# Four first loads moved to GpSimd's queue, the first batch's order list rearranged, two pieces of work moved to GpSimd

## The chip, the cores and the metric

The kernel runs on one core of a Trainium2 chip. The metric is device time in microseconds of one execution; medians of several executions are quoted, and comparisons use runs of the same rounds on the same chip. A profile is one execution under the hardware profiler; its "span" is some 1.8 us shorter than the time measured for the same execution. Names of engines: PE is TensorE, PEld its weight loads, DVE is VectorE, ACT is ScalarE, POOL is GpSimd, SP is SyncE; a name with q added (SPq) is that engine's queue of issues.

## The reference, cut to what matters

Eight batches of attention with RMS-normalised queries and keys (12 heads, 448 positions, 64 dimensions), then a layer norm and a two-layer MLP with a residual.

```python
batch, n_heads, seq, head_dim = (8, 12, 448, 64)
def rmsnorm(x, g):
    return x / np.sqrt(np.mean(x * x, axis=-1, keepdims=True) + 1e-06) * g
q_n, k_n = (rmsnorm(q, g_q), rmsnorm(k, g_k))
scores = (1.0 / np.sqrt(head_dim)) * np.matmul(q_n, k_n.transpose(0, 1, 3, 2))
attn = softmax(scores)                       # written out in the original
x = np.matmul(attn, v)                       # heads joined: (8, 448, 768)
xn = (x - mean(x)) / np.sqrt(var(x) + 1e-06) * g_ln
out = x + np.maximum(xn @ w_ch1, 0.0) @ w_ch2     # w_ch1 768x3072, w_ch2 3072x768
```

## The kernel before

Heads are worked on in pairs, and pairs are prepared in "units" (pair 0, pair 1, pairs 2 and 3, pairs 4 and 5 of batch 0, then two pairs each). To prepare a unit, its keys and queries are squared (`a`, `c`, ScalarE), summed (`d`, `e`, VectorE), put through an inverse square root (`g`, ScalarE), the keys are weighted with g_q·g_k (`i`) and split into an fp16 high part (`j`) and low part (`k`), the queries are scaled and duplicated (`l`, `m`), the values cast to fp16 (`z`, GpSimd). Then `K` and `Q` are the PE transposes of a pair's keys and queries, `S` a tile of scores with its exponential, `V` a tile of values, `N`, `X` and `R` the layer norm of batch 0 and its transposes, `U` the first MLP products. The other letters (`b`, `G`, `L`, `T`, `W`, `A`, `M`) stand for setting up a unit, later loads and small steps that the argument doesn't need. For batch 0 an explicit list gives the order in which all of this is issued to the in-order engines:

```python
DVE_KG, POOL_HI, POOL_DUP, ACT_Q = (0, 1, 2), (1, 2, 3, 4), (1, 2, 4), (0, 1)
ORDER = """
b0 a0 c0 G L4 L5 i0 j0 e0 k0 gq0 l0 b1 m0 a1 c1 K0 Q0 d0 gk0 S0.0 S0.1 i1 e1 d1 g1 z0 j1 l1 m1
k1 b2 a2 S0.2 c2 S0.3 d2 K1 e2 S0.4 V0.0 i2 S0.5 Q1 g2 j2 l2 V0.1 S0.6 S1.0 S1.1 S1.2 m2 b3
...   # cut
S6.6 X0 X1 U0 V6.5 c5 N2 X2 d5 U1 U2 R e5 V6.6 g5 j5 k5 l5 m5 z5 L7 M
""".split()
...
        def kg():                            # "i", line 229
            if u == 0:
                nc.vector.tensor_tensor(out=sh.gprod, in0=sh.gg[:, 0], in1=sh.gg[:, 1],
                                        op=ALU.mult)          # line 227
            (nc.vector if u in DVE_KG else nc.gpsimd).tensor_tensor(
                out=c["t"][1], in0=c["t"][1],
                in1=sh.gprod.unsqueeze(1).broadcast_to([128, g, D]), op=ALU.mult)

        def khi():                           # "j", line 235 or 237
            if u in POOL_HI:
                nc.gpsimd.tensor_copy(out=c["khl"][:, :, 0], in_=c["t"][1])
            else:
                nc.scalar.activation(c["khl"][:, :, 0], c["t"][1], AFT.Identity)
```

The first loads. `main` loads a pair's first 384 rows, `left` the last 64, in two halves:

```python
        for n, eng in ((0, nc.sync), (1, nc.scalar)):      # queries, keys
            main(eng, n, 0)
            left(eng, n, 0, 1)
        left(nc.scalar, 1, 1, NPAIR - 1)
        for n in range(2):
            nc.sync.dma_start(self.sh.gg[:, n], self.gs[n].unsqueeze(0).broadcast_to([128, D]))
        main(nc.sync, 1, 1)
        ...                                                # cut: SyncE's further loads
```

## Time and profile before

| what | before |
|---|---|
| time, median of 3 runs | 616.35 us (615.82 to 616.48) |
| span of the profile | 613.9 us |
| PE busy | 581.3 us, 95% |
| ScalarE busy | 362.0 us, 59% |
| VectorE busy | 289.8 us, 47% |
| GpSimd busy | 185.7 us, 30% |

Read such a table with care: PE is busy 95% over the whole run, but two thirds of its 33 us of idle time lie in the first 60 us, where the other engines are the limit, and the change concerns only that stretch. The prediction below therefore starts from the table by stretches and from what PE waited for.

### The profile page before, as it was taken

The numbers are of one execution on the slowest core, as the hardware profiler recorded it, in microseconds if no ns is written. First come the engines' busy times: TensorE is split into PE (matmuls) and PEld (weight loads), VectorE is DVE, ScalarE is ACT, GpSimd is POOL, SyncE is SP. The second block draws the span as 40 slices with busy tenths as digits, with TensorE's granted clock in tenths as the row PEclk, the third lists the DMA queues.
The fourth block names the chain that finished last, engine by engine and source line by source line (L and its number), as shares of the span: only waits on it lengthen the run. The fifth ranks groups of instructions, "written<-read, shape, count | busy, mean of one in ns | idle before, by whom it ended". The sixth has DMA issues, their size and how long they took to land.

```text
span 613.9 us, 11521 instructions
## 1 busy us (share of the span) xinstructions
PE 581.3 (95%) x4500; PEld 346.2 (56%) x4500; DVE 289.8 (47%) x615; ACT 362.0 (59%) x697; POOL 185.7 (30%) x239
## 2 busy tenths in 40 slices
PE   2777999999999999999999999999999999999995
PEld 1545566655566666655566666655566666654564
DVE  4798766733356355643356355642355422440011
ACT  4897886438754498538755398537765377114200
POOL 0646432224452155514453145605322000000000
PEclk9999999999999999999999999999999999999998
DMA  7999799655536467847659495836524330030011
GB/s 185 289 177 230 151 222 224 135 157 123 121 102 132 98 142 152 179 108 144 111 102 141 105 137 151 176 105 150 117 61 87 91 61 2 27 104 0 1 52 56
DMA packets 131661, 75.29 MB, mean 123 GB/s; under 512 B 97552, under 2 KB 121904, under 8 KB 131600
## 3 DMA queue, kind: packets, MB, share of 16 engines
q1 hardware_dynamic: 114336, 45.18, 35.2%
q0 software_dynamic: 15920, 28.71, 21.2%
q8 instruction: 37, 0.61, 0.4%
q10 hardware_dynamic: 1344, 0.59, 0.4%
q14 instruction: 24, 0.20, 0.1%
HBM read 52.36 MB, written 11.01 MB: 103 GB/s over the span
## 4 chain that ended last, share of the span: by engine, by line
PE 87%; DVE 4%; ACT 4%; issue 1%; ACTq 0%; DVEq 0%
PE psC L627 35%; PE psH L611 34%; PE psS L352 8%; PE oA L381 5%; PE oB L383 2%; ACT E L358 1%; PE psS L355 1%; PE psS L356 1%; DVE ssq L218 1%; DVE x L398 1%; ACT qn L215 1%; PE tr L316 1%; DVE khl L240 1%; DVE qU L335 0%; DVE xn L560 0%
## 5 line engine op out<-in xcount | busy, mean ns | idle before, releaser
L611 PE MATMUL psH<-xnT,w 128*128 128x512 f16 (+1 forms) x1134 | 242.1, 353 | 0.4 <-issue 0.4
L358 ACT ACTIVATE E<-psS,rr_all 128x448 f16<-128x448 f32 x336 | 207.2, 635 | 50.0 <-PE psS L352 44.1
L627 PE MATMUL psC<-w,hT 128*128 128x384 f16 (+1 forms) x1368 | 234.7, 323 | 0.0
L613 ACT ACTIVATE hT<-psH 128x512 f16<-128x512 f32 (+1 forms) x189 | 104.0, 551 | 126.2 <-PE psH L611 123.3
L627 PEld LDWEIGHTS <-hT 128*128 128x128 f16 x1368 | 127.7, 98 | 74.2
L611 PEld LDWEIGHTS <-w 128*128 128x128 f16 x1134 | 102.5, 98 | 81.4 <-issue 1.5
L352 PE MATMUL psS<-qU,kU 128*128 128x448 f16 x288 | 101.7, 360 | 8.0 <-ACT E L358 6.0
L381 PEld LDWEIGHTS <-E 128*128 128x128 f16 x1008 | 71.1, 99 | 50.3 <-issue 4.4
L229 POOL TENSOR_TENSOR qkv<-qkv,gprod 128x896 f32<-128x896 f32 x21 | 43.7, 2079 | 99.2 <-ACT khl L215 51.6
L381 PE MATMUL oA<-v,E 128*128 128x65 f16 x864 | 67.2, 194 | 0.9 <-DVE x L398 0.8
L631 DVE SCALAR_TENSOR_TENSOR x<-psC,rs_all,x 128x384 f32<-128x384 f32 x48 | 29.0, 616 | 70.8 <-PE psC L627 70.3
L396 DVE RECIPROCAL rec_all<-oA 128x6 f32<-128x6 f32 x48 | 9.3, 194 | 98.1 <-PE oA L381 98.0
L383 PE MATMUL oB<-v,E 128*128 128x65 f16 x288 | 52.1, 195 | 0.1
L127 POOL DMA_DIRECT2D qkv<-in_k_dram x14 | 11.2, 800 | 131.2 <-ACT E L358 68.6
L218 DVE TENSOR_REDUCE ssq<-khl 128x14 f32<-128x896 f32 (+1 forms) x24 | 25.5, 1064 | 43.9 <-ACT khl L215 43.8
L352 PEld LDWEIGHTS <-kU 128*128 128x128 f16 x288 | 28.2, 99 | 25.6 <-issue 7.2
L218 DVE TENSOR_REDUCE ssq<-qn 128x14 f32<-128x896 f32 (+1 forms) x25 | 26.2, 1047 | 22.9 <-ACT qn L215 22.8
L67 DVE SCALAR_TENSOR_TENSOR qn<-qkv,rq 128x256 f16<-128x256 f32 (+1 forms) x72 | 26.9, 430 | 18.7 <-ACT rq L223 18.5
L383 PEld LDWEIGHTS <-E 128*128 128x128 f16 x336 | 32.7, 97 | 0.5 <-DVE xl L403 0.2
L398 DVE TENSOR_TENSOR x<-oA,rec_all 128x384 f32<-128x384 f32 x48 | 26.8, 558 | 1.7 <-DVE rec_all L397 0.2
L240 DVE TENSOR_TENSOR khl<-qkv,khl 128x896 f16<-128x896 f32 x21 | 22.8, 1083 | 7.9 <-ACT khl L237 7.9
L540 DVE BATCH_NORM_STATS2 stat<-x 128x6 f32<-128x256 f32 x72 | 26.1, 415 | 0.7
(101 smaller groups left out, 447.9 us busy)
## 6 DMA issues: line engine op xcount, KB each, us to landing
out_dram<-x SPq DMA_DIRECT2D x20, 384.0 KB, 2.5
qkv<-in_k_dram POOLq DMA_DIRECT2D x14, 384.0 KB, 3.9
qkv<-in_q_dram POOLq DMA_DIRECT2D x14, 384.0 KB, 5.2
qkv<-in_v_dram POOLq DMA_DIRECT2D x14, 384.0 KB, 6.0
w<-in_moe_w_ch_dram POOLq DMA_DIRECT2D x3, 1536.0 KB, 12.0
w<-in_moe_w_ch_dram POOLq DMA_DIRECT2D x2, 2304.0 KB, 26.9
qkv<-in_k_dram SPq DMA_DIRECT2D x7, 384.0 KB, 5.6
qkv<-in_q_dram SPq DMA_DIRECT2D x7, 384.0 KB, 4.9
```

The lines of the kernel that those rows point to most:

```text
L218: nc.vector.tensor_reduce(out=c["ssq"][:, n], in_=c["sq", n], axis=AX.X, op=ALU.add)
L229: (nc.vector if u in DVE_KG else nc.gpsimd).tensor_tensor(out=c["t"][1], in0=c["t"][1], in1=sh.gprod.unsqueeze(1).broadcast_to([128, g, D] ...
L240: nc.vector.tensor_tensor(out=c["khl"][:, :, 1], in0=c["t"][1], in1=c["khl"][:, :, 0], op=ALU.subtract)
L352: nc.tensor.matmul(ps[:, 0:S], c["main"][:, ts(i, 128)], q[:, ts(h, S)], start=True, stop=True)
L358: nc.scalar.activation(out=c["E"][:, i], in_=ps[:, 0:S], func=AFT.Exp, scale=self.rr[:, g:g + 1], bias=EXP_BIAS)
L381: nc.tensor.matmul(oA[:, t, cs], E[:, i, ts(t, 128)], rhs, start=(i == 0 and t == 0), stop=(i == 6 and t == 2))
L383: nc.tensor.matmul(oB[:, cs], E[:, i, 320:448], rhs, start=(i == 0), stop=(i == 6))
L398: nc.vector.tensor_tensor(out=x[:, :, 128 * hp:128 * hp + 128].rearrange("p t (e d) -> p t e d", e=2), in0=oA[:, :, :, 0:D], in1=rec[:, 0: ...
L611: nc.tensor.matmul(ps[:, 0:N], sh.w1[:, dc, ts(f, 128)], xnT[:, dc, 0:N], start=(dc == 0), stop=(dc == NDC - 1))
L613: nc.scalar.activation(out=hT[:, f, 0:N], in_=ps[:, 0:N], func=AFT.Relu)
L627: nc.tensor.matmul(ps[:, 0:g[1]], hT[:, f, ts(t, 128)], sh.w2[:, f, cols], start=(f == 0), stop=(f == NFF - 1))
L631: nc.vector.scalar_tensor_tensor(out=x[:, cols], in0=ps[:, 0:g[1]], scalar=self.rs[:, b, t:t + 1], in1=x[:, cols], op0=ALU.mult, op1=ALU.add)
```

## The change

The intent is to let the first key transpose start sooner by spreading the first issues over three queues, and to feed PE better up to the first MLP by a better order of issue and by taking work from VectorE and ScalarE to GpSimd. `DVE_KG` without 2 puts the key weighting of unit 2 on GpSimd; `POOL_HI` with 5 puts the fp16 conversion of unit 5's keys there.

```diff
-DVE_KG, POOL_HI, POOL_DUP, ACT_Q = (0, 1, 2), (1, 2, 3, 4), (1, 2, 4), (0, 1)
+DVE_KG, POOL_HI, POOL_DUP, ACT_Q = (0, 1), (1, 2, 3, 4, 5), (1, 2, 4), (0, 1)
 ORDER = """
-b0 a0 c0 G L4 L5 i0 j0 e0 k0 gq0 l0 b1 m0 a1 c1 K0 Q0 d0 gk0 S0.0 S0.1 i1 e1 d1 g1 z0 j1 l1 m1
-k1 b2 a2 S0.2 c2 S0.3 d2 K1 e2 S0.4 V0.0 i2 S0.5 Q1 g2 j2 l2 V0.1 S0.6 S1.0 S1.1 S1.2 m2 b3
...  (middle cut)
-S6.6 X0 X1 U0 V6.5 c5 N2 X2 d5 U1 U2 R e5 V6.6 g5 j5 k5 l5 m5 z5 L7 M
+G b0 a0 c0 L4 L5 i0 j0 e0 k0 gq0 l0 b1 m0 a1 c1 K0 Q0 d0 gk0 S0.0 S0.1 i1 e1 d1 z0 g1 j1 l1 m1
+k1 b2 a2 S0.2 d2 c2 S0.3 S0.4 K1 V0.0 e2 i2 S0.5 Q1 g2 l2 S0.6 S1.0 j2 V0.1 S1.1 S1.2 m2 b3
...  (middle cut)
+S6.6 V6.4 X0 X1 U0 N2 d5 j5 R X2 c5 e5 g5 k5 z5 l5 L7 V6.5 U1 U2 M m5 V6.6
@@ load_first @@
-        left(nc.scalar, 1, 1, NPAIR - 1)
         for n in range(2):
-            nc.sync.dma_start(self.sh.gg[:, n], self.gs[n].unsqueeze(0).broadcast_to([128, D]))
+            nc.gpsimd.dma_start(self.sh.gg[:, n], self.gs[n].unsqueeze(0).broadcast_to([128, D]))
+        left(nc.gpsimd, 1, 1, NPAIR - 1)
```

## The prediction

> **What bounds the kernel now.** I read the busy time by stage first, because an average over the whole run hides where TensorE (PE) is idle. These are rows of the table by stretches of the kernel before (stretch, its length, busy time of PE, of PE's weight loads, of VectorE, ScalarE and GpSimd, then clock, DMA share, GB/s):
>
> ```profile
> 0.00:10.00 10.00, 0.00 (x0) 0.00 (x0) 3.56 (x14) 3.58 (x8) 0.68 (x6) 1.00 0.55 133
> 10.00:20.00 10.00, 5.46 (x32) 3.04 (x33) 7.42 (x13) 6.72 (x15) 2.80 (x5) 1.00 1.09 306
> 20.00:30.00 10.00, 9.35 (x89) 6.20 (x88) 8.02 (x11) 9.48 (x19) 6.66 (x7) 1.00 0.90 268
> 30.00:40.00 10.00, 8.58 (x115) 5.78 (x113) 9.62 (x20) 9.51 (x19) 5.43 (x7) 1.00 1.00 188
> 40.00:50.00 10.00, 7.10 (x89) 4.44 (x88) 9.59 (x21) 9.09 (x19) 5.16 (x7) 1.00 1.05 189
> 50.00:60.00 10.00, 7.36 (x108) 5.69 (x108) 8.44 (x16) 6.78 (x12) 6.33 (x5) 1.00 1.11 255
> ...
> 60.00:120.00 60.00, 56.75 (x505) 36.47 (x504) 42.04 (x84) 45.95 (x93) 19.31 (x18) 1.00 1.00 188
> 120.00:200.00 80.00, 79.44 (x567) 44.53 (x565) 36.58 (x76) 46.73 (x86) 29.77 (x39) 1.00 0.51 125
> 200.00:500.00 300.00, 300.00 (x2288) 177.81 (x2287) 138.44 (x304) 190.29 (x371) 109.58 (x147) 1.00 0.60 123
> ```
>
> From 60 us on PE is the bound: 3.3 us idle up to 120, 0.6 up to 200, none up to 500. In the first 60 us it is idle 10.0 + 4.5 + 0.7 + 1.4 + 2.9 + 2.6 = 22.1 us. PE's work is not changed, so a microsecond of PE idle saved in the first 60 us is a microsecond off the end, unless a later wait eats it. The change touches only that stage: its bound is the whole game, and 22.1 us is far more than can be had.
>
> What PE waits for there, from the table of waits (what waited, for what; us in total, times, longest):
>
> ```profile
> PE tr L313 <- DVE khl L240: 13.1, 2, 10.1
> PE psS L352 <- ACT E L358: 6.0, 18, 0.6
> ...
> DVE gprod L227 <- DMA w<-in_g_k_dram: 5.0, 1, 5.0
> ```
>
> So there are three parts: 10.1 us before the first key transpose, 3.0 us before the second (18.29), then many short waits for ScalarE's exponentials, with ScalarE 95% and VectorE 96% busy from 30 to 40. The first is a chain that I follow in the timeline (start, duration, what):
>
> ```profile
> 2.78 0.59 SPq L151 DMA_DIRECT2D w<-in_g_q_dram  x1
> 4.31 0.33 SPq L151 DMA_DIRECT2D w<-in_g_k_dram  x1
> 4.66 1.28 ACT L417 ACT_TABLE_LOAD   x1 [4.66 <-DMA hT<-in_q_dram]
> ...
> 7.84 0.23 DVE L227 TENSOR_TENSOR gprod<-w 128x64 f32<-128x64 f32 x1 [4.96 <-DMA w<-in_g_k_dram]
> ...
> 14.83 0.82 POOL L285 CAST v<-w 128x768 f16<-128x768 f32 x1 [13.52 <-DMA w<-in_v_dram]
> ...
> 17.29 0.94 DVE L240 TENSOR_TENSOR khl<-hT,khl 128x448 f16<-128x448 f32 x1 [1.16 <-POOL khl L235]
> ```
>
> The weights g_q and g_k are the fourth and fifth issues of SyncE's queue. g_k goes out at 4.31, lands 3.5 us later, the product is formed at 7.84, and key weighting (8.15), high part (8.81) and low part (9.42) follow back to back to PE's first transpose at 10.10. ScalarE meanwhile issues six key transfers until 4.63, and only then loads its table. The second wait is GpSimd's: pair 0's values land at 14.83, the conversion of unit 1's keys stands behind them (16.70), VectorE waits for that (17.29), PE for VectorE.
>
> **What the Trainium skill says.** "DMA: Bandwidth & Descriptors", section "Issuing engines are not separate DMA queues", says that spreading issues over engines saves sequencer issue time only. The trace agrees that issue time is what is scarce here: SyncE issues from 0.74 to 16.66 almost without a gap, while the DMA engines are busy only 55% in the first 10 us. Its section "Latency and other measured facts" gives a first byte at about 0.6 us on the SyncE/ScalarE path and 1 us on GpSimd's. No transfer of this size on GpSimd's queue is in the trace; the nearest, halves of left rows, take 0.60 us to issue and 3.0 us or more to land, beside 3.1 to 3.7 on SyncE's and ScalarE's. "GPSIMD Engine Reference", section "Engine selection", calls elementwise work with two inputs about twice as slow there: here the same key weighting takes 2.08 us on GpSimd and 1.08 on VectorE, so it agrees. "SBUF — State Buffer", section "Who interferes with whom", says that a VectorE instruction with two SBUF inputs contends with a GpSimd one that reads SBUF. The trace agrees: a query scaling of 1.08 us took 1.71 at 22.28 beside a GpSimd cast, and a GpSimd copy of 0.93 us took 1.66 at 24.12.
>
> **The change part by part.**
>
> *Key and query weights on GpSimd's queue.* GpSimd has finished the identity at 1.31 and has nothing until 14.83. Two issues of 0.6 to 0.9 us go out at about 1.3 and 2.1, and land 3.0 to 3.9 us later (the 3.9 is the median of whole key loads on that queue): 5.1 to 6.0, so the product is ready at about 5.4 to 6.3, beside 8.07 before. The key weighting works in place and so also waits for the keys' square on ScalarE, below.
>
> *Left key rows of later pairs off ScalarE.* ScalarE's issues end about 2.6 instead of 4.63 (two issues, and the pause before the last). The table load then ends near 3.9, the first small Ln near 4.2. The square can begin when pair 0's left keys are there: second half issued near 1.95, landing 3.1 later, 5.05; it ends near 5.7 (it began at 6.07 and ended at 6.63 before). So weighting starts at about 6.1, beside 8.15: **2.0 us earlier**, and with it PE's first transpose, at about 8.1. The moved rows are issued from GpSimd at about 2.9 and 3.5 and land near 7 to 8; pair 1's square reads them at 9.69 before, about 7.7 after. That is close, but it costs a few tenths at most.
>
> *SyncE's queue.* It loses two issues (2.78 and 4.31). What follows moves from 4.69 up by 1.1 to 1.9 us: less if the pause of 0.94 us before 4.31 stays and falls on another transfer. Issue to landing is 4 to 5 us, so pair 0's values land 1.1 to 1.9 earlier, and the second PE wait moves by as much: the lead is kept, not doubled.
>
> *Unit 2's key weighting.* VectorE loses 1.08 us at 20.83; GpSimd gains 2.08 us, in a stretch where it is idle 4.4 us (17.76 to 22.12). The converted keys can start when they did or earlier. From 27.7 to 45 the chain that ended last runs mainly on VectorE, so part of the 1.08 counts; ScalarE is as full in that stretch, so not all: I take 0.4.
>
> *The rearranged list.* The clear step is that score tile S0.4 goes ahead of the second key transpose K1. Before, it stood behind it, and ScalarE sat idle 1.79 us at 19.63. One exponential (0.53 us) now fits into that gap. The rest of ScalarE's time from 22 to 48 has about 1.5 us idle, so reordering can win little. Later, unit 5's key square sum comes before the copy of the third transposed tile (VectorE waits 1.55 us there), and its conversion leaves ScalarE for GpSimd (0.93 us at 61.0, near the end of the thin stage). I take 0.3 for the list up to 48 and 0.3 for the later part. Moving the load of the layer norm weight to the front changes nothing: it is queued after all the first loads in both kernels.
>
> Sum: 2.0 + 0.4 + 0.3 + 0.3 = 3.0 us. From this I take 0.2, as the loads of the later weights come closer to their readers: 2.8 us off 616.35 gives **613.5 us**.
>
> **The rivals.**
> *The lead is lost again:* ScalarE from 22 to 54 has hardly a gap, so it carries a lead through rather than eats one, but if the first values or pair 1's queries come no earlier (the DMA engines show a share of 1.09 from 10 to 20), only some 1 us is left: 615.3. For it speaks that share; against it, that those transfers take 4 to 5 us however full the engines are, so issue order sets them.
> *GpSimd's queue starts slowly:* it has never been used before 29.26, and VectorE's memsets run until 2.87. If its first transfer took 3 us more, the product would be formed no earlier than before, and all waits stay: 616 to 617.5. Its first use at 29.26 took 1.01 us to issue, which speaks against it.
> *Contention:* the new 2.08 us on GpSimd beside VectorE's two-input instructions can stretch either by 0.6 to 0.7 us, as seen at 22.28 and 24.12. It would cost up to half a microsecond: 614.
> *The search of the order pays more:* PE's idle time from 30 to 57 is about 6.5 us. If the new list recovers 2 us of it, 611.5.
> *Later weights become the wait:* between 70 and 110 the DMA engines are the fullest, and the second-layer weights' first half takes 24 us or more after its issue at 67.34, for use at 95.4. If it lands no sooner, a lead of over some 4 us would be cut off; mine is smaller.
>
> **Range and chances.** The mechanism's size rests on GpSimd's landing time (0.9 us wide), on SyncE's shift (0.8 us wide), and on what the list does to the two full engines (about 2 us either way). So 8 in 10: 610.8 to 616.2. 2% is 12.3 us: more than half of all PE idle in the first 60 us would have to go, though 10 to 57 is mostly ScalarE's bound, and nothing makes the kernel slower by as much. Faster 0.01, same 0.975, slower 0.015.
>
> **What would show it right or wrong.** Right: the product at about 5.5 to 6.3 and PE's first transpose at about 8.1; ScalarE's table load near 2.6; pair 0's values cast at about 13; the second key transpose wait gone or moved by 1 to 2 us; unit 2's weighting as a fifth unit on GpSimd at 2.08 us; PE idle to 60 us down from 22.1 to about 19; the last stretches unchanged but shifted. Wrong: a product later than 7, a new PE wait on values or on unit 2's keys, VectorE instructions stretched beside GpSimd, or a wait of the second-layer products for their weights near 95.

## More of the kernel before

From pair 6 on, the transposes of a pair's keys and queries share one PSUM tile (`self.tr`, which PE's transposes write), so a `Q` waits until VectorE has copied the `K` out of it:

```python
    def trans_k(self, p):
        kT, ps = self.kU[PE_SET][:, 960 * (p % 2):960 * (p % 2) + 960], self.tr
        ...                                                # cut: seven PE transposes
        nc.vector.tensor_copy(out=kT, in_=ps[:, 0:960])    # line 318

    def trans_q(self, p):
        tr = self.ps_m.tile([128, 1024], FP16, tag="mlp", name="psQ") if p < NPAIR else self.tr
```

And from unit 8 on, keys and queries are transposed by DMA on SyncE's queue (eight transfers a unit, "x" and "y"), on which the transposes of the normalised rows of batch 1 (`xnT`) are issued too:

```python
            for x, names in enumerate(pieces):             # "pieces" ends with ..., "x", "y"
                at = st + (e - st) * x // (k - 1) if x < k else e + 1 + x - k
```

## The result, and the profile after

The changed kernel took 614.99 us (median of 4 runs, 614.82 to 615.52) beside 616.4 us for the kernel before (4 runs, 615.82 to 616.48). The ratio is 0.9981 (95% interval 0.9963 to 0.9998), class "same" (within 2%). Ratios here are the mean time of one kernel's fast runs over the mean of the other's of the same rounds, so not quite the ratio of the quoted medians. In a second set of rounds (e4 below) it was 0.9972, so the gain is 1.2 to 1.7 us. The time lies inside the predicted range, but the predicted gain, 2.8 us, was about twice the measured one.

The table by stretches of the changed kernel (columns as in the prediction):

```profile
0.00:10.00 10.00, 1.43 (x13) 1.23 (x14) 4.97 (x16) 4.78 (x9) 3.30 (x10) 1.00 0.78 181
10.00:20.00 10.00, 5.78 (x30) 2.82 (x28) 6.53 (x10) 7.29 (x15) 6.08 (x7) 1.00 1.12 305
20.00:30.00 10.00, 9.15 (x95) 6.45 (x94) 7.04 (x11) 9.42 (x19) 7.18 (x8) 1.00 0.89 252
30.00:40.00 10.00, 8.09 (x106) 5.54 (x105) 9.59 (x21) 9.79 (x20) 5.50 (x8) 1.00 0.93 165
40.00:50.00 10.00, 7.37 (x88) 4.32 (x87) 9.52 (x23) 8.75 (x18) 6.47 (x7) 1.00 1.12 212
50.00:60.00 10.00, 8.46 (x121) 6.73 (x118) 9.44 (x20) 6.81 (x16) 2.97 (x4) 1.00 1.02 235
60.00:120.00 60.00, 55.47 (x494) 35.69 (x492) 39.69 (x77) 43.72 (x85) 19.30 (x18) 1.00 1.00 186
120.00:200.00 80.00, 78.81 (x563) 44.12 (x561) 35.92 (x76) 46.73 (x86) 29.76 (x39) 1.00 0.59 125
```

PE's idle time up to 60 us is 19.7 us, 2.4 less than before: close to what was predicted. But from 60 to 120 it is 4.5 us instead of 3.3, and from 120 to 200 it is 1.2 instead of 0.6. So 1.9 of the 2.4 us came back as idle time later, in stages that the change was not meant to touch. What PE waited for (us in total, times, longest) names the two places:

```profile
PE tr L313 <- DVE khl L240: 10.4, 3, 8.6
...
PE tr L327 <- DVE kU L318: 1.2, 1, 1.2
PE psH L611 <- DMA xnT<-xn: 1.1, 1, 1.1
```

The first key transpose still begins late (8.6 us), but earlier than before, and the second wait is the short one. The other two rows were not in the kernel before's table: a query transpose waits for VectorE's copy of the keys out of the shared PSUM tile (before, PE was idle 0.04 us there), and the first layer of batch 1 waits for its DMA-transposed input. That second wait is not wholly new: before, PE was idle 0.43 us there.

One profile is one execution, and PE's matmuls become fast (0.53 us to 0.35 us for one 128x448 score matmul) at a moment that varied from 20 to 29 us between the profiles, whatever the kernel. So I compare three profiles of each plain kernel. Times of the milestones in us, means of three:

| milestone on PE or VectorE | before | changed | lead |
|---|---|---|---|
| first key transpose | 10.18 | 8.69 | 1.5 |
| second key transpose (K1) | 18.48 | 17.04 | 1.4 |
| third key transpose (K2) | 25.24 | 22.86 | 2.4 |
| layer norm of batch 0 begins (VectorE) | 52.11 | 50.37 | 1.7 |
| first MLP product (U0) | 55.40 | 52.84 | **2.6** |
| query transpose of pair 7 (Q7) | 62.02 | 60.96 | **1.05** |
| first second-layer product | 95.11 | 94.05 | 1.06 |
| first layer of batch 1 | 128.66 | 128.04 | **0.6** |
| end of the span | 613.97 | 613.07 | 0.9 |

The lead is 2.6 us at 53 us, loses 1.5 by Q7, and is near 1 from there on; from 130 us to 500 PE is busy all the time in both. The loss of 1.5 us is no chance of single profiles: from U0 to Q7 it took 6.61 to 6.62 us in each profile of the kernel before and 8.12 in each of the changed one.

### The profile page after: what moved, and what is told of

It is laid out like the page before. It is cut to its first block, busy times and chain, and to the rows that moved or that the text cites. A ratio compares the mean times of both kernels' runs of the same rounds, so it can differ in the third digit from the quotient of the medians.

```text
span 613.8 us, 11526 instructions
## 1 busy us (share of the span) xinstructions
PE 581.6 (95%) x4500; PEld 346.8 (57%) x4500; DVE 287.2 (47%) x614; ACT 361.4 (59%) x696; POOL 190.1 (31%) x245
## 4 chain that ended last, share of the span: by engine, by line
PE 84%; DMA 5%; DVE 5%; ACT 3%; SPq 1%; issue 1%; POOL 0%; DVEq 0%; ACTq 0%; POOLq 0%
PE psH L611 33%; PE psC L627 33%; PE psS L352 8%; PE oA L381 5%; DMA qkv<-in_k_dram 2%; PE oB L383 2%; ACT E L358 2%; DMA hT<-in_k_dram 1%; PE psS L355 1%; PE psS L356 1%; DVE khl L240 1%; DMA hT<-in_q_dram 1%; ACT qn L215 1%; DVE x L398 1%; DVE qn L67 1%
## 5 line engine op out<-in xcount | busy, mean ns | idle before, releaser
L67 DVE SCALAR_TENSOR_TENSOR qn<-qkv,rq 128x256 f16<-128x256 f32 (+1 forms) x72 | 26.9, 431 | 19.3 <-ACT rq L223 19.3
```

The source lines that it names most:

```text
L67: nc.vector.scalar_tensor_tensor(out=out, in0=x, scalar=8.0, in1=r.unsqueeze(2).broadcast_to([x.shape[0], g, D]), op0=ALU.mult, op1=ALU.mult)
```

## The experiments

Each was made from the kernel before or the changed one as said.

**Which part gives what: the loads alone, the two GpSimd jobs alone, the list alone, and the changed kernel again.** e1 is the kernel before with only the last part of the diff, e2 with only the `DVE_KG` and `POOL_HI` line, e3 with only the new list.

> Kernel before with the loads part alone (weights and later left key rows on GpSimd's queue; order list and unit 2 and 5 as before). Theory A (the start gives 1.5 us, and it is eaten only where later stages are bound by something fixed): first PE transpose at 8.57 instead of 10.10, second key transpose at about 17.0 instead of 18.29, lead about 1.3 us at 50 us and at 95 us, time 0.7 to 1.4 us below before. Rival B (the start's lead is lost in the DMA-bound stretch whatever the order): less than 0.4 us below before.

> Kernel before with unit 2's key weighting and unit 5's conversion on GpSimd alone (order list and loads as before). Theory A (unit 5's conversion holds GpSimd's value casts back[...]): the three layer norm instructions take 2.9 us instead of 3.85, value casts 1.5 to 0.9 us; time 0.3 to 1.2 us below before. Rival: the conversion only leaves ScalarE and the layer norm stays at 3.85 us, time within 0.3 us of before.

> Kernel before with the new order list alone. Theory A: the exponential of S0.4 comes before K1 (0.3 to 0.4 us gained by 22 us), but late in the list the division of pair 6 and the query copies stand ahead of pair 7's key copy on VectorE, so PE waits about 1 us near 60 us; sum within 0.5 us of before either way. Rival (the list is where the gain comes from): over 1 us below before.

> The changed kernel once more, unedited, timed in five rounds and profiled anew, because its profiled run was its slowest and that of before its fastest: 1.0 to 1.6 us below before in time. If the wait of the second batch's first layer for its transposed input (1.1 us at 128 us) is regular, the new profile has it again; if it is a chance of that run, it is under 0.6 us.

| run | median us (before 615.58) | ratio to before | 95% interval |
|---|---|---|---|
| e1, loads alone | 614.37 | 0.9984 | 0.9964 to 1.0004 |
| e2, GpSimd jobs alone | 617.79 | 1.0032 | 1.0013 to 1.0052 |
| e3, list alone | 618.79 | 1.0049 | 1.0032 to 1.0066 |
| e4, all (changed kernel) | 614.00 | 0.9972 | 0.9955 to 0.9989 |

By these estimates the loads alone give most of the measured gain (1.0 of 1.2 to 1.7 us), though the interval of e1 just takes in no gain. My expectation came true for e1 and e4; for e2 (0.3 to 1.2 us gained) and e3 (within 0.5 us of before) it did not. The other two parts each **cost** 2 to 3 us alone, and together, with the loads, they cost nothing: they do not add, so a sum over parts was the wrong form for them. In e2 the query transpose Q7 waited 2.2 us. In e3 PE waited 1.7 us for ScalarE's relu of the first products, whose queue held unit 5's conversion in its new, earlier place; 1.0 us at Q7 came on top.

**The list and the GpSimd jobs with the old loads.** e11 is the changed kernel with the old `load_first`.

> Changed kernel with the loads as before (so order list and GpSimd's work together, without the loads part). Theory (the two belong together: each alone cost 2 to 3 us, together they give the rest of the gain): 0.3 to 1.0 us below before; layer norm at 2.9 us. Rival (they cost and the loads carry everything): slower than before.

615.37 us, ratio 0.9992 (0.9978 to 1.0007). Its profile shows where the gain of list and jobs stays: U0 is at 53.68, 1.7 us before the mean of the kernel before, but Q7 is at 61.79 after a wait of 1.16 us, only 0.2 ahead. In e1, which has the old list, U0 is at 54.12 and Q7 at 60.74 without a wait: the loads alone reach Q7 as early as the changed kernel does. What list and jobs win up to U0, 1.3 us between e1 and the mean of the changed kernel, is gone at Q7.

**Where that gain came from: the layer norm.** Before, VectorE's three layer-norm instructions (two inputs in SBUF) ran beside GpSimd's value casts of unit 5. VectorE and GpSimd of the kernel before in the timeline (start, duration, engine and line):

```profile
52.38 3.85 DVE L560 SCALAR_TENSOR_TENSOR xn<-x,stat,gln 128x768 f16<-128x768 f32 x3
...
52.91 1.54 POOL L285 CAST v<-qkv 128x768 f16<-128x768 f32 x1
54.41 1.98 POOL L291 CAST vl<-qkv 64x128 f16<-64x128 f32 x2
```

The same in the changed kernel:

```profile
50.93 2.88 DVE L560 SCALAR_TENSOR_TENSOR xn<-x,stat,gln 128x768 f16<-128x768 f32 x3
...
54.96 0.93 POOL L235 CAST khl<-qkv 128x896 f16<-128x896 f32 x1 [5.05 <-DVE ssq L218]
55.84 0.83 POOL L285 CAST v<-qkv 128x768 f16<-128x768 f32 x1
```

The conversion that moved to GpSimd may only overwrite the squares of the keys after VectorE has summed them, so GpSimd's queue now stands idle for 5.05 us until the layer norm is over, and the casts behind it run alone. The layer norm falls from 3.85 to 2.88 us and the cast from 1.54 to 0.83; PE gains 0.8 us of this (from the start of the layer norm to U0, 3.3 us before, 2.5 in the changed kernel, in all three profiles of each). In e1 (old list and jobs) the layer norm still took 3.86 us, in e11 2.88. The move of the conversion was expected to help ScalarE; what it did was to act as a gate. The gate is one way to this, not the only one: with the old list it gave 3.26 us (e2, and e14 below), and with the new list but without it, in e3, the same casts ran before the layer norm (52.57 to 53.97) and it took 3.00 us.

**Which of the two GpSimd jobs costs, and in which list.** e12 is the changed kernel with unit 2's weighting back on VectorE; e13 and e14 are the kernel before with one job moved.

```diff
-DVE_KG, POOL_HI, ... = (0, 1), (1, 2, 3, 4, 5), ...      # changed
+DVE_KG, POOL_HI, ... = (0, 1, 2), (1, 2, 3, 4, 5), ...   # e12, from the changed kernel
-DVE_KG, POOL_HI, ... = (0, 1, 2), (1, 2, 3, 4), ...      # before
+DVE_KG, POOL_HI, ... = (0, 1), (1, 2, 3, 4), ...         # e13, from the kernel before
+DVE_KG, POOL_HI, ... = (0, 1, 2), (1, 2, 3, 4, 5), ...   # e14, from the kernel before
```

> Changed kernel with unit 2's key weighting back on VectorE. Theory (1.08 us on VectorE near 19 us, before VectorE is full, counts for at most half): 0.2 to 0.8 us above the changed kernel, with the exponentials from 22 us on later by that much. Rival (the 2.08 to 2.45 us on GpSimd cost as much as they save): no difference.

> Kernel before with unit 2's key weighting alone moved to GpSimd. Theory: K2's transposes come 0.4 us earlier (24.6 instead of 25.05), ScalarE's exponentials hardly move, time within 0.6 us of before. Rival: this is the part that costs 2 us in the old list.

> Kernel before with unit 5's conversion alone moved to GpSimd. Theory: the layer norm takes 3.0 to 3.3 us instead of 3.85, but the program that is built then puts unit 5's low part and query scaling ahead of pair 7's key copy on VectorE, and PE waits about 2.2 us for that copy near 61 us: 1.0 to 2.5 us above before. Rival: it gains, and unit 2's weighting costs.

- e12: 617.36 us, ratio 1.0019 (1.0006 to 1.0033): by the ratios 2.3 to 2.9 us worse than the changed kernel (0.9981 and 0.9972), where I had expected under 1. Two rows of its timeline show where it begins:

```profile
20.93 1.68 POOL L235 CAST khl<-hT 128x896 f16<-128x896 f32 x1 [4.36 <-DMA qkv<-in_k_dram]
...
22.64 1.79 DVE L240 TENSOR_TENSOR khl<-hT,khl 128x896 f16<-128x896 f32 x1 [0.83 <-POOL khl L235]
```

The changed kernel has these two as

```profile
19.02 0.93 POOL L235 CAST khl<-hT 128x896 f16<-128x896 f32 x1
...
21.70 1.08 DVE L240 TENSOR_TENSOR khl<-hT,khl 128x896 f16<-128x896 f32 x1
```

With the weighting on VectorE, the conversion starts 1.9 us later and falls beside VectorE's two-input query scaling (20.72). It takes 0.75 us more, and so does the low part (0.71), which falls beside GpSimd's copy and cast. The third key transpose comes at 24.48 instead of 23.00, and ScalarE stands idle 0.75 and 1.36 us after it. So the trace shows 1.5 us of the loss; in this one profile PE also became fast as late as 28.9 us, and how the rest divides is not shown.
- e13: 615.45 us beside 615.74, ratio 1.0001 (0.9984 to 1.0017), as expected: in the old list the same move is worth nothing.
- e14: 617.39 us, ratio 1.0026 (1.0009 to 1.0043), as expected: in the old list the earlier conversion brings VectorE's low part (60.24) and query scaling (61.31) ahead of the copy that Q7 waits for (62.42). It is this job that makes e2 slow.

**The start: the two load moves one by one.** e9 has only g_q and g_k on GpSimd, e10 only the left rows, e15 both with the left rows first.

```diff
-            nc.sync.dma_start(self.sh.gg[:, n], ...)      # e9, e15 (e15 after the left rows)
+            nc.gpsimd.dma_start(self.sh.gg[:, n], ...)
-        left(nc.scalar, 1, 1, NPAIR - 1)                  # e10, e15
+        left(nc.gpsimd, 1, 1, NPAIR - 1)
```

> Kernel before with only g_q and g_k moved to GpSimd's queue; the later pairs' left key rows stay on ScalarE. Theory (the start is now set by pair 0's left keys landing near 6.0 to 6.2, so the table load's 2.2 us lead buys nothing): product near 6.4, square of the keys at 6.0 to 6.2, first PE transpose at 8.5 to 8.9, as with both moves; time as the loads part alone, 1.0 us below before. Rival (both moves are needed, as the prediction on record has it): first transpose later than 9.2.

> Kernel before with only the later pairs' left key rows moved to GpSimd's queue. Theory: table load at 2.5 instead of 4.66, but the square still waits for the landing near 6.1 and the product for g_k until 7.4 or later: first transpose 9.6 to 10.1, time within 0.4 us of before. Rival: the first transpose comes earlier by over half a microsecond.

> Loads part alone, but on GpSimd's queue the later left key rows go out ahead of g_q and g_k. Theory (the weights' transfers, 256 rows of 256 bytes, delay pair 0's left keys): square of the keys at 5.3 to 5.6 instead of 6.0 to 6.4, but product near 7.5 to 7.9, first PE transpose near 9.8. Rival (any early transfer from GpSimd delays them): square still at 6.0 or later.

| us | table load | first square (keys) | g product | first key transpose | time, ratio |
|---|---|---|---|---|---|
| before | 4.66 | 6.07 | 7.84 | 10.10 | |
| e9, weights | 4.55 | 5.96 | 6.22 | 8.50 | 614.42, 0.9975 (0.9962 to 0.9987) |
| e10, left rows | 2.50 | 5.33 | 6.59 | 8.86 | 615.54, 0.9993 (0.9980 to 1.0005) |
| e1, both | 2.50 | 6.21 | 6.44 | 8.77 | 614.37, 0.9984 |
| e15, both, left rows first | 2.50 | 5.63 | 7.26 | 9.53 | 614.39, 0.9999 (0.9973 to 1.0024) |

The two moves do not add: each alone starts PE 1.2 to 1.6 us earlier, and so do both. The reason is in the timeline of the changed kernel (the number in brackets is the idle time before, and what ended it):

```profile
2.38 0.56 POOL L150 DMA_DIRECT2D w<-in_g_k_dram  x1
2.50 1.28 ACT L417 ACT_TABLE_LOAD   x1 [2.50 <-issue]
...
6.01 0.58 ACT L215 ACTIVATE hT<-hT 128x448 f32<-128x448 f32 x1 [2.02 <-DMA hT<-in_k_dram]
6.26 0.23 DVE L227 TENSOR_TENSOR gprod<-w 128x64 f32<-128x64 f32 x1 [3.39 <-DMA w<-in_g_k_dram]
...
8.57 0.29 PE L313 MATMUL tr<-id,khl 128*128 128x128 f16 x1 [8.57 <-DVE khl L240]
```

ScalarE is free 2 us earlier and then waits 2.02 us for pair 0's keys, so its square comes only 0.06 us earlier than before. Where the weights' issues come after the left rows (e15) or stay on SyncE (e10), the keys land 0.4 to 0.7 us earlier, but the weights later. The issue that the square waits for is ScalarE's last of pair 0's keys, at 1.86. The view of DMA issues around it gives its time to landing, in the kernel before and in the changed one (KB, us):

```profile
hT<-in_k_dram ACTq DMA_DIRECT2D x1, 16.0 KB, 3.0
...
hT<-in_k_dram ACTq DMA_DIRECT2D x1, 16.0 KB, 4.0
```

The repeats of the two kernels have 3.1 and 3.2, and 4.2 twice. It is 3.4 us in e10, 3.7 in e9 and in e15, and 4.2 in e1 (one profile each): it grows with what GpSimd issues beside it. I had expected e10 to start PE at 9.6 to 10.1; it started at 8.86, because SyncE's pause before its second weight went away with ScalarE's issues (issue at 3.42, before 4.31). That part of my theory fell. e10's time shows less than its start, but its profile was its slowest run and in it PE ran slow once more near 55 us (18 matmuls in 2.13 us, elsewhere 1.42). e15's time is inconclusive: one of its four runs was 617.66. Its first transpose is late, but its second, K1, came at 16.09, the earliest of all profiles (16.67 to 17.32 in the others with both moves), and its first second-layer product at 92.53, before the changed kernel's 94.05. So the first transpose alone does not tell the worth of an order of loads; I have one profile of this one, of its fastest run, and did not follow it.

**The transposes of batch 1.** Unit 8's query transposes are issued six steps later, so that those of `xnT` come before them; e5 from the changed kernel, e6 from the kernel before.

```diff
                 at = st + (e - st) * x // (k - 1) if x < k else e + 1 + x - k
+                at += 6 * (u == DMA_UNIT and names == "y")
```

> Changed kernel, but unit 8's query transposes are issued from SyncE's queue six steps later, so that the second batch's normalized tiles are transposed ahead of them. Theory (the end of the lead is cut at 128 us because those transposes stand in SyncE's queue): the wait of the first layer for them goes to 0, first layer of batch 1 starts about 1 us earlier relative to the end of the batch before, time 0.5 to 1.1 us below the changed kernel. Rival (VectorE's chain to the normalized tiles or the DMA engines set it): change under 0.3 us.

> Kernel before with the same delay of unit 8's query transposes. Theory: before, the second batch's first layer waited only 0.43 us there, so it gains about 0.4 us; rival: nothing, or as much as the changed kernel gains.

SyncE's queue in the kernel before, then SyncE's queue and PE in the plain changed kernel:

```profile
110.32 2.43 SPq L258 DMA_TRANSPOSE kU<-khl  x1
...
122.28 5.23 SPq L586 DMA_TRANSPOSE xnT<-xn  x4
```

```profile
109.57 3.36 SPq L258 DMA_TRANSPOSE kU<-khl  x1
...
122.08 5.23 SPq L586 DMA_TRANSPOSE xnT<-xn  x4
...
128.75 1.46 PE L611 MATMUL psH<-xnT,w 128*128 128x512 f16 x6 [1.06 <-DMA xnT<-xn]
```

In the kernel before, the `xnT` transposes begin at 122.28, only 0.2 us later, although PE is then 0.8 us behind (95.38 against 94.61 at the first second-layer product): the first key transpose of unit 8 took 2.43 us there (3.17 and 2.21 in its repeats; 3.36, 3.29 and 3.01 in the three profiles of the changed kernel). The queue carries no lead through, and PE waits for it 1.06 us. With the edit, e5 took 613.97 us beside 616.04, ratio 0.9960 (0.9942 to 0.9979), and e6 614.29, ratio 0.9968 (0.9949 to 0.9987). In both profiles the wait is gone (first layer of batch 1 at 126.97 and 127.62). So this queue was a limit in **both** kernels. That weakens my account of this loss: with the queue out of the way in both, the changed kernel should regain its lead over the other, and e5 is only 0.3 us under e6 by the medians, 0.5 by the means. The trace shows the wait; the time does not show that it took the lead. Also e6 gained 1.75 us, and its trace accounts for 0.6 of it (33.5 us down to 32.9 from the first second-layer product to batch 1's first layer); the rest is open.

**Q7.** The shared PSUM tile is filled and emptied earlier: K7 goes ahead of the value tile, Q7 ahead of the division of pair 6, at the end of the list. e7 from the changed kernel, e8 with the edit of e5 as well.

```diff
-S6.6 V6.4 X0 X1 U0 N2 d5 j5 R X2 c5 e5 g5 k5 z5 l5 L7 V6.5 U1 U2 M m5 V6.6
+S6.6 V6.4 X0 X1 U0 N2 d5 j5 R X2 c5 e5 g5 k5 z5 l5 K7 L7 V6.5 U1 U2 Q7 M m5 V6.6
```

> Changed kernel with pair 7's key and query transposes put ahead of the last value products and of unit 5's query copy in the list, so that VectorE copies them before the division of pair 6. Theory (1.1 us of the lead is lost at 60 us because PE waits for that copy): the wait of 1.16 us at 61.5 us is gone, second layer starts near 93.6 instead of 94.6 us, time 0.4 to 1 us below the changed kernel, less if the wait at 128 us eats it. Rival (VectorE's work up to there is what counts, whatever its order): the wait moves to the next scores and nothing is gained.

> Both edits on the changed kernel. Theory: both leaks closed, 1.5 to 2 us below the changed kernel, near 613.2 us, as much as the prediction on record had hoped for. Rival: one of the two is absorbed by the other, 0.5 to 1 us below.

In the kernel before, the copy comes in time, and PE hardly waits at Q7 (0.04 us):

```profile
61.57 0.66 DVE L318 COPY kU<-tr 128x960 f16<-128x960 f16 x1
...
62.28 0.22 PE L327 MATMUL tr<-id,qn 128*128 128x128 f16 x1
```

In the changed kernel VectorE's division of pair 6 stands ahead of the copy, and PE waits for the copy:

```profile
59.89 0.56 DVE L398 TENSOR_TENSOR x<-oA,rec_all 128x384 f32<-128x384 f32 x1
...
60.81 0.66 DVE L318 COPY kU<-tr 128x960 f16<-128x960 f16 x1
...
61.52 0.22 PE L327 MATMUL tr<-id,qn 128*128 128x128 f16 x1 [1.16 <-DVE kU L318]
```

In e7:

```profile
55.05 0.22 PE L313 MATMUL tr<-id,khl 128*128 128x128 f16 x1 [0.71 <-DVE xnT L598]
...
58.03 0.64 DVE L318 COPY kU<-tr 128x960 f16<-128x960 f16 x1
...
58.73 0.22 PE L327 MATMUL tr<-id,qn 128*128 128x128 f16 x1 [0.28 <-DVE kU L318]
```

e7 took 612.06 us beside 616.04, ratio 0.9930 (0.9911 to 0.9949). The wait at Q7 falls by 0.88 us, a new one of 0.71 appears before K7, and with the queries ready earlier 0.5 us of PE's waits for exponentials between 56 and 100 us, 0.34 for a relu at 57.86 and 0.82 for a division at 99.82 go as well: the first second-layer product comes at 91.83 instead of 94.05. e8 took **611.24 us** (610.91 to 611.47), ratio 0.9918 (0.9899 to 0.9937): 4.8 us under the kernel before by the medians, 2.7 under e5, and the best version. PE's idle time from 60 to 120 is 1.9 us in it and from 120 to 200 0.1 us. Not all of this is a return of what the change lost: the wait at 99.8 was there in the kernel before too (0.82 at 100.59). Both gains are larger than I had expected (e7 0.4 to 1 us below the changed kernel, e8 near 613.2 us). The edit moves PE's transposes forward together with VectorE's copies, and it was not tried on the kernel before.

**More profiles of the two plain kernels**, for the milestones above: e16 and e18 are the kernel before, e17 the changed one, one look each.

> Kernel before, unedited, one more profile. Expectation: matmuls become fast anywhere from 20 to 29 us; first second-layer product between 94.6 and 95.9 us and first layer of batch 1 between 128.2 and 129.5 us, later in step with a later speed-up.

> Changed kernel, unedited, one more profile on the same chip: second layer between 93.9 and 94.7 us, first layer of batch 1 between 127.9 and 128.8 us, with a wait of 0.9 to 1.2 us there; 0.5 to 1 us ahead of before at a like moment of speed-up.

> Kernel before, unedited, again: as the first repeat; the spread of the two shows how much of a difference between single profiles is chance (some 0.7 us).

615.74, 614.13 and 615.82 us. These are single runs, of unknown state; the run of the kernel before beside them took 617.75, so no ratio is made of them. e17's milestones fell outside what I had expected of them: 93.54 and 127.33 us, each 0.4 to 0.6 earlier, and a wait of 0.70. The repeats show that the first pair of profiles, with spans only 0.1 us apart, was unlucky: one kernel's profiled run was 0.7 us under its median (615.66), the other's 0.5 over it (615.52).

## Why the prediction was right or wrong, point by point

- **The bound, and a microsecond of idle time for a microsecond of time: right, with its condition.** PE's work did not change, and what is left of the lead at 130 us (0.6) is near what the end shows (0.9). But the condition, "unless a later wait eats it", came true: of 2.4 us of idle time saved, 1.9 came back.
- **The start, 2.0 us earlier: mis-sized, it was 1.5** (1.2 by all 17 profiles with old or new loads that were read for it). The failed step is "The square can begin when pair 0's left keys are there: second half issued near 1.95, landing 3.1 later, 5.05". The landing took 4.0 us instead of 3.1, and the square began at 6.01: with the weights' transfers from GpSimd in flight the keys of pair 0 land later; with the weights left on SyncE (e10) the square began at 5.33. The product, predicted ready at 5.4 to 6.3, was formed from 6.26 to 6.49, near the late end. ScalarE's earlier table load was seen (2.50) and bought nothing.
- **SyncE's queue: right.** Values cast at 13.69 (1.1 earlier), second transpose 1.4 earlier (means of three): the lead is kept.
- **Unit 2's weighting 0.4, the list 0.3 + 0.3: the sum was about right up to 55 us (1.3 against 1.0), by luck; the terms were not.** They cannot be given to the parts one by one: unit 2's weighting is worth about 2.5 us in the new list (e12) and nothing in the old (e13), the list alone costs 3 us. The lead was already 2.4 us at K2, near 23 us, and 1.7 at the layer norm. The list's "clear step" came true and won nothing there: with the same new loads, S0.4's exponential starts at 16.21 us in the changed kernel and at 18.00 in e1, which has the old list, but ScalarE then stands idle 1.80 us (in e1 1.50, ahead of S0.4), and the next exponential starts at 18.64 against 18.60. And 0.8 us of the gain is the layer norm freed of GpSimd's casts, which the prediction did not foresee; it named contention as a cost only.
- **"From this I take 0.2, as the loads of the later weights come closer to their readers": this is the step that failed most.** A lead of 2.6 us was there at U0, close to the 2.8 foretold, and 1.5 of it was lost within 8 us. That is not a matter of later weights: no wait for them appears. 1.1 us of it was VectorE's order at the copy before Q7 (PE's wait there 1.16 us against 0.04; U0 to Q7 took 8.11 us in e11, with list and jobs but old loads, and 6.62 in e1, with new loads alone; e7 undoes it). The other 0.4 was lost before K7, 0.34 of it in a wait for ScalarE's relu at 57.86. Another 0.4 us was lost on SyncE's queue at batch 1 by the traces, which the times of e5 and e6 do not confirm. The prediction read the list only up to U0 and took the rest as "unchanged but shifted"; "unless a later wait eats it" was said, and then not looked for where the list's own tail had been rearranged.
- **The rivals.** "GpSimd's queue starts slowly" did not come true; nor did "Later weights become the wait". The idle time that "The search of the order pays more" counts from 30 to 57 us was 7.0 us, not 6.5; the new list alone lost time (e3). "Contention" was real but went the other way: relieved at 52 us more than it cost at 16.51, where unit 2's weighting took 2.45 us instead of 2.08, and the conversion behind it still began 3.1 us earlier than before (19.02 against 22.12). "The lead is lost again" named nearly the right size (615.3) for another reason.

Open: what made e6 gain more than its trace shows; why the first DMA transpose of unit 8 takes from 2.1 to 4.0 us, and even in profiles of one kernel from 2.2 to 3.2; and what e7's edit is worth without the change.

## What to carry to other kernels

A lead won at the start must be followed through every in-order queue up to the stage where the bounding engine runs without gaps: here VectorE's order at one copy took 1.1 of 2.6 us, and moving that copy with its transposes gave back more than the whole change had won. Parts of a rearranged schedule are to be judged together, since list and GpSimd jobs here each cost 2 to 3 us in the other's absence. A GpSimd instruction that has to wait can keep GpSimd's further copies off a stretch in which VectorE has two-input work; look at what runs beside the instruction, not only at what is ahead of it.

## What the Trainium skill lacked or had wrong

- "DMA: Bandwidth & Descriptors", section "Latency and other measured facts", gives a first byte at about 1 us for GpSimd's queue and a fixed cost of some 2 us for a DMA. It has no figure for a small load beside others in flight: the weights' loads, 32 KB each, took 0.73 and 0.56 us to issue and landed 3.7 and 3.8 us after the start of issue.
- "DMA: Bandwidth & Descriptors", section "Issuing engines are not separate DMA queues", says that several issuing engines save sequencer time only, and that their transfers interleave on the same DMA engines. The runs agree; what it lacks is how much of the time saved this can cost at such a start: the last of pair 0's keys landed 3.0 us after issue before and 4.0 in the changed kernel, and they were used at 5.33 us with the weights on SyncE's queue (e10), 5.63 with them late on GpSimd's (e15), and 6.01 and 6.21 with them early on it (changed kernel and e1).
- "SBUF — State Buffer", section "Who interferes with whom": the runs agree and add sizes. Layer norm 3.85 against 2.88 us for three instructions; the low part of the keys 1.79 against 1.08; a GpSimd cast of 128x768 1.54 against 0.83; a GpSimd weighting of 128x896 2.45 against 2.08.
- "TensorE: Matmul & The Clock Gate", section "Part 1: The HAM clock gate (the "warmup" mystery)", says that PE becomes fast after some 3.4 us of sustained activity, counted in windows that run free of the kernel's work. Here PE's first work was at 8.5 to 10.2 us, and the score matmuls went from 0.53 to 0.35 us only at 20 to 29 us, while the clock column of the tables reads 1.00 throughout. In the kernel before, PE worked without a pause from 18.29 to 22.46 us and from 22.92 on, and its transposes became faster (0.31 to 0.24 us each) only near 26.9. Work of 4.2 us may still miss a full window, so this does not contradict the page, but no run here shows the windows. For work with pauses it has no figure, and the moment varied by up to 9 us between runs.
